# Last row of layer 2: its normalising factor by a square root on ScalarE and a reciprocal on VectorE instead of a power on GpSimd

## The chip, the cores and the metric

One core of one Trainium2 chip. The metric is the device time of one execution of the kernel in microseconds; lower is better. Engines are named as in the profile: PE is TensorE's matmul, PEld its weight load, DVE VectorE, ACT ScalarE, POOL GpSimd, SP SyncE, which here only issues transfers. A "q" behind an engine's name is its instruction queue.

## The reference

Four residual layers on one sequence of 2048 rows of 576 numbers, in float32. Layers A mix by discrete Fourier transforms, written as products with given cosine and sine matrices; layers B gate the layer-normed rows with a long convolution that does not depend on `x`.

```python
def _layernorm(x, axis=-1, eps=1e-5):
    m = jnp.mean(x, axis=axis, keepdims=True)
    v = jnp.var(x, axis=axis, keepdims=True)
    return (x - m) / jnp.sqrt(v + eps)

def _A_ref(x, dft_seq_re, dft_seq_im, dft_hid_re, dft_hid_im):
    a = jnp.einsum("bsd,ed->bse", x, dft_hid_re)
    b = jnp.einsum("bsd,ed->bse", x, dft_hid_im)
    return jnp.einsum("ts,bse->bte", dft_seq_re, a) - jnp.einsum("ts,bse->bte", dft_seq_im, b)

def _B_ref(q, k, v, shift_k, ssm_k, ssm_D):
    ...            # short convolution of k, times v, long convolution by FFT: y
    return q * y

x = A_x
x = x + _A_ref(_layernorm(x, axis=-1), A_dft_seq_re, A_dft_seq_im, A_dft_hid_re, A_dft_hid_im)
x = x + _B_ref(_layernorm(x, axis=-1), B_k, B_v, B_shift_k, B_ssm_k, B_ssm_D)
x = x + _A_ref(_layernorm(x, axis=-1), A_dft_seq_re, A_dft_seq_im, A_dft_hid_re, A_dft_hid_im)
x = x + _B_ref(_layernorm(x, axis=-1), B_k, B_v, B_shift_k, B_ssm_k, B_ssm_D)
```

## The kernel before, in words

The 2048 rows lie as 16 tiles of 128 partitions by 576 numbers; the code calls one tile a row `j`, from 0 to `J - 1` = 15. Every float32 product is made of products of rounded halves: `split` (lines 97 to 99) writes the rounded half on ScalarE (line 98) and the remainder on VectorE (line 99).

A layer A first multiplies by the sequence matrices, streamed in from memory block by block, then by the 576x576 hidden matrices (`hidden`, lines 276 to 289). The first pass of the kernel also computes the long convolution of layer B once, beside TensorE's work, and stores it in `yb_d`. The second pass saves matmuls over the sequence matrices by a Strassen scheme (`strassen`, lines 952 to 1008). The very last stage is the loop at lines 1066 to 1074: for each of four blocks and each of the four rows in it, `hidden` runs two halves of 288 columns of 27 matmuls each, adds each half to the residual (line 287), and then calls `done1` (lines 735 to 744), which does the last layer B and sends the row out.

`done1` uses `gated` (lines 656 to 670). It loads the convolution's row, gets mean and variance through `norm_stats` (lines 177 to 185), forms (x − mean) · y on VectorE (line 665), multiplies by the factor and adds the residual (line 668). `norm_stats` takes the statistics of two halves (line 181), joins them (line 182), adds epsilon (line 183) and raises to the power −0.5 on GpSimd (line 184). For the last row alone, `last` is given: line 668 then runs in two halves of 288 columns, and the first half is sent by ScalarE's queue, the second by SP's (line 739). The other rows are sent whole by SP (line 744).

Small numbers live in the tile `flts`: the constant −0.5 in column 0 (`mhalf`), and four `stat` slots of 20 columns that are used in turn. Line 175 is a first activation on ScalarE, in front of all work. Some rows of the first pass and the second layer take their statistics by `sums` (lines 646 to 654), with a Copy and a Square on ScalarE instead of line 181.

The order of instructions on an engine is laid out when the kernel is built, from the program and its dependences; in places the source fixes it with `tc.issue_after` (`behind`, lines 102 to 106). So it need not be the source's order: `f1_loads` (line 416) stands in the source ahead of the first split in `f1_split`.

Of the kernel before, what the change touches and what calls it, by code (L numbers as in the profile page):

```python
# [12 lines left out]
AF = mybir.ActivationFunctionType  # L13
OP = mybir.AluOpType
# [8 lines left out]
HD = D // 2  # L23
NC = 4
REM = D - NC * P
EPS = 1e-5
# [39 lines left out]
def fnet_h3_kernel(ctx: ExitStack, tc: tile.TileContext, x, c_mat, w_re, w_im, k_pad, v, shift_k,  # L66
                   ssm_k, ssm_d, f1c, i2c, midc, out):
    nc = tc.nc
# [43 lines left out]
    def flat(words, dt, name):  # L112
        return sb.tile([P, words], dt, tag=name, name=name)
# [15 lines left out]
    ring = {}  # L129

    def lay(t, at, *sizes):

        for name, words, n in sizes:
            ring.setdefault(name, Ring()).tiles.extend(t[:, at + i * words:at + (i + 1) * words] for i in range(n))
            at += n * words
        assert at <= t.shape[1], (at, t.shape, sizes)
        return at
# [16 lines left out]
    um = []  # L154

    flts = flat(FLT, F32, "flts")
    mhalf = flts[:, :1]
    lay(flts, 8, ("stat", STAT, 4))
    lay(flts, RT_AT, ("rt", NT, 1))
    lay(mats, X_END, ("cs", WIDE, 3))  # L160
# [5 lines left out]
    def load_after(dst, src):  # L166
        with tc.issue_after(anchor[-1]):
            return nc.sync.dma_start(dst, src).ins
# [3 lines left out]
            nc.gpsimd.dma_start(dst, src)  # L172

    nc.vector.memset(mhalf, -0.5)
    nc.scalar.activation(flts[:, 1:2], mhalf, AF.Copy)

    def norm_stats(src):
        m = ring["stat"]()
        st, mv, ve, rs = m[:, :12].rearrange("p (a c) -> p a c", a=2), m[:, 12:14], m[:, 14:15], m[:, 15:16]
        for i in range(2):  # L180
            nc.vector.bn_stats(st[:, i, :], src[:, i * HD:(i + 1) * HD])
        nc.vector.bn_aggr(mv, st)
        nc.vector.tensor_scalar(ve, mv[:, 1:2], EPS, None, op0=OP.add)  # L183
        pows.append(nc.gpsimd.tensor_tensor(rs, ve, mhalf, OP.pow).ins)  # L184
        return mv, rs, m[:, 16:17]
# [460 lines left out]
    def sums(src, junk):  # L646
        m = ring["stat"]()
        sm, sv, rs, nb = (m[:, i:i + 1] for i in range(4))
        nc.scalar.activation(junk, src, AF.Copy, accum_out=sm)
        nc.vector.tensor_scalar(sm, sm, -1.0 / D, None, op0=OP.mult)  # L650
        nc.scalar.activation(junk, src, AF.Square, bias=sm, accum_out=sv)
        nc.vector.tensor_scalar(sv, sv, 1.0 / D, EPS, op0=OP.mult, op1=OP.add)
        pows.append(nc.gpsimd.tensor_tensor(rs, sv, mhalf, OP.pow).ins)
        return sm, rs, nb

    def gated(xa, q, j, junk=None, last=None):
        load_after(q, yb_d[j])
        if junk is None:
            mv, rs, _ = norm_stats(xa)
            mean, op = mv[:, 0:1], OP.subtract  # L660
        else:
            mean, rs, _ = sums(xa, junk)
            op = OP.add
        yield
        nc.vector.scalar_tensor_tensor(q, xa, mean, q, op0=op, op1=OP.mult)
        for i in range(2 if last else 1):
            cs = slice(i * HD, (i + 1) * HD) if last else slice(None)
            nc.vector.scalar_tensor_tensor(q[:, cs], q[:, cs], rs, xa[:, cs], op0=OP.mult, op1=OP.add)
            if last:
                last(i, cs)  # L670

# [35 lines left out]
    def make_x1(j):  # L707
        xa, q = ring["xa"](), ring["yb"]()
        load_after(xa, xa_d[j])
        for _ in gated(xa, q, j, ring["xj"]() if j % 2 and j >= EARLY else None):  # L710
            yield
        for _ in normed_x(q, xa, ring["xj"]()):
            to_store.append((xb_d[j], q))
            yield
        to_store.append((y_d[j // 2][:, j % 2, :], xa))
        X[j] = to_x(xa, j)
        ready.add(j)
# [17 lines left out]
    def done1(j, xa):  # L735
        q = ring["yb"]()

        def store(i, cs):
            (nc.scalar if i == 0 else nc.sync).dma_start(out[:, j, cs], q[:, cs])

        for _ in gated(xa, q, j, last=store if j == J - 1 else None):
            pass
        if j < J - 1:
            nc.sync.dma_start(out[:, j, :], q)
# [27 lines left out]
    for n, whole in layer(get_x0, lambda j: x[:, j, :], done0, pending):  # L772
# [30 lines left out]
        m = n - PREP  # L803
# [138 lines left out]
    cs, done = {}, []  # L942
# [212 lines left out]
```

## Time and profile before

| | |
|---|---|
| median of 3 runs | 1190.23 us |
| the three runs | 1188.69, 1190.23, 1192.36 us |
| the profiled execution: time / span | 1191.32 / 1189.5 us |
| mean granted TensorE clock | 0.998 |
| busy share of the span | PE 98%, DVE 73%, ACT 55%, POOL 6% |
| power on GpSimd, line 184 | 35 times, 0.547 to 1.055 us, the last at 1183.3 us |

The profile shows one execution. The span is the time from its first to its last instruction; the device time contains some more around it. In rows of the timeline the first number is the start, the second the duration, both in us, then engine, line, operation, what is written and read, and the shape; a bracket gives the idle time of the engine before and what ended it. In rows of groups, the numbers behind the first bar are the summed busy time in us and the mean of one in ns, those behind the second the idle time before them.

### The profile page before, as it was taken

The page shows a single profiled execution, that of the slowest core. Times are in us where ns is not written, and L with a number is a line of the kernel's source. Part 1 is how long each engine was busy: PE and PEld are TensorE (multiplying, and loading weights), DVE is VectorE, ACT ScalarE, POOL GpSimd, SP SyncE. Part 2 cuts the span into 40 slices and gives each one's busy share as a digit, 9 for nine tenths or more (in the row PEclk, how much of TensorE's full clock was granted, in tenths as well). Part 3 has the DMA queues.
Part 4 walks back from the last instruction along what each step waited for, and adds up shares of the span by engine and source line. Part 5 has one row for each costly group of instructions (what it writes and reads, how often), then busy time and mean ns, then how long its engine had stood idle before and what let it go on. Part 6 is the DMA issues. An engine that isn't in the chain of part 4 may idle for free.

```text
span 1189.5 us, 18071 instructions
## 1 busy us (share of the span) xinstructions
PE 1168.5 (98%) x6184; PEld 987.2 (83%) x6184; DVE 872.8 (73%) x1562; ACT 650.0 (55%) x1279; POOL 75.1 (6%) x116
## 2 busy tenths in 40 slices
PE   7999999999999999999999999999999999999997
PEld 5776767888888888888888898888888888889997
DVE  7899983688777778787767665865776776775764
ACT  7865555567766668766645666534444445450200
POOL 2210000000000000001101111000000000001111
PEclk9999999999999999999999999999999999999999
DMA  9869898545656656648966777772772776795621
GB/s 340 295 197 306 269 290 267 178 139 177 225 189 198 200 160 204 186 137 239 273 197 226 235 246 231 251 250 73 255 248 71 240 273 248 266 322 158 214 83 41
DMA packets 147454, 255.65 MB, mean 215 GB/s; under 512 B 16161, under 2 KB 56353, under 8 KB 147362
## 3 DMA queue, kind: packets, MB, share of 16 engines
q1 hardware_dynamic: 111890, 210.17, 54.9%
q10 hardware_dynamic: 28560, 37.91, 9.1%
q0 software_dynamic: 6912, 6.43, 2.4%
q8 instruction: 48, 0.79, 0.3%
q14 instruction: 44, 0.36, 0.1%
HBM read 187.80 MB, written 66.65 MB: 214 GB/s over the span
## 4 chain that ended last, share of the span: by engine, by line
PE 76%; ACT 2%; DVE 2%; DMA 2%; issue 1%; POOLq 0%; ACTq 0%; DVEq 0%
PE s L75 42%; PE bk L75 29%; PE rm L75 4%; ACT flts L512 1%; ACT mid L512 1%; DMA t<-ud 1%; DVE mid L518 0%; DMA yb<-flts 0%; DMA flts<-vd 0%; DMA flts<-in_c_mat 0%; DVE flts L532 0%; DVE flts L530 0%; ACT u L98 0%; DVE flts L531 0%; DVE flts L533 0%
## 5 line engine op out<-in xcount | busy, mean ns | idle before, releaser
L75 PE MATMUL s<-mats 128*128 128x512 f32 x2088 | 543.0, 395 | 1.6 <-ACT mats L195 0.8
L75 PEld LDWEIGHTS s<-mats 128*128 128x128 f32 x2088 | 381.0, 188 | 83.2 <-issue 10.6
L99 DVE TENSOR_TENSOR mats<-flts,mats 128x512 fp32r<-128x512 f32 x206 | 141.0, 688 | 50.8 <-ACT mats L98 48.4
L98 ACT ACTIVATE mats<-flts 128x512 fp32r<-128x512 f32 x206 | 128.3, 628 | 82.6 <-PE bk L75 31.2
L75 PE MATMUL bk<-mid 128*128 128x288 f32 x704 | 127.7, 302 | 1.6 <-DVE flts L287 0.8
L75 PEld LDWEIGHTS bk<-mid 128*128 128x128 f32 x704 | 108.0, 188 | 23.7 <-ACT flts L512 5.8
L512 ACT ACTIVATE flts<-bk 128x288 f32<-128x288 f32 (+1 forms) x192 | 76.3, 406 | 90.8 <-PE bk L75 75.9
L75 PE MATMUL bk<-w,u 128*128 128x288 f32 x864 | 121.3, 296 | 1.0 <-DVE w L241 0.4
L75 PEld LDWEIGHTS bk<-w,u 128*128 128x128 f32 x864 | 117.3, 188 | 5.5 <-DVE flts L532 1.7
L518 DVE TENSOR_TENSOR mid<-flts,mid 128x576 fp32r<-128x576 f32 (+1 forms) x149 | 93.4, 629 | 18.6 <-ACT mid L512 15.2
L75 PE MATMUL rm<-mats 128*128 128x512 f32 x304 | 94.6, 391 | 0.2 <-ACT flts L512 0.2
L512 ACT ACTIVATE mid<-flts 128x576 fp32r<-128x576 f32 (+1 forms) x148 | 80.3, 575 | 11.8 <-DVE flts L533 8.5
L287 DVE TENSOR_TENSOR flts<-flts,bk 128x288 f32<-128x288 f32 x48 | 21.8, 453 | 65.8 <-PE bk L75 65.7
L451 ACT ACTIVATE flts<-bf 128x384 f32<-128x384 f32 (+1 forms) x104 | 43.2, 463 | 46.0 <-PE bf L75 45.9
L75 PE MATMUL bk<-mats 128*128 128x288 f32 (+1 forms) x376 | 67.8, 317 | 0.0
L75 PEld LDWEIGHTS rm<-mats 128*128 128x128 f32 x304 | 56.9, 188 | 12.8 <-ACT flts L512 0.6
L75 PE MATMUL s<-t,mats 128*128 128x512 f32 x264 | 65.4, 390 | 0.6 <-DVE t L99 0.3
L184 POOL TENSOR_TENSOR flts<-flts 128x1 f32<-128x1 f32 x35 | 28.7, 821 | 522.4 <-DVE flts L183 522.3
L75 PE MATMUL bk<-mats,t 128*128 128x288 f32 (+1 forms) x368 | 59.3, 303 | 0.0
L512 ACT ACTIVATE flts<-flts 64x288 f32<-64x288 f32 x128 | 56.6, 443 | 4.7
L75 PEld LDWEIGHTS s<-t,mats 128*128 128x128 f32 x264 | 49.4, 188 | 11.7 <-DVE t L99 0.8
L75 PEld LDWEIGHTS bk<-mats 128*128 128x128 f32 x376 | 55.5, 188 | 3.4
(146 smaller groups left out, 1496.7 us busy)
## 6 DMA issues: line engine op xcount, KB each, us to landing
flts<-in_c_mat SPq DMA_DIRECT2D x148, 256.0 KB, 3.3
ph<-in_c_mat SPq DMA_DIRECT2D x54, 512.0 KB, 4.5
flts<-in_c_mat SPq DMA_DIRECT2D x30, 512.0 KB, 4.8
flts<-td SPq DMA_DIRECT2D x53, 288.0 KB, 2.9
td<-flts ACTq DMA_DIRECT2D x36, 384.0 KB, 4.6
vd<-flts ACTq DMA_DIRECT2D x64, 144.0 KB, 2.7
flts<-vd SPq DMA_DIRECT2D x32, 288.0 KB, 4.1
ud<-ph ACTq DMA_DIRECT2D x12, 512.0 KB, 6.3
```

What stands on the lines that cost most here:

```text
L75: return nc.tensor.matmul(ps, lhsT, rhs, start=first, stop=last, skip_group_check=more).ins
L98: a = nc.scalar.activation(h, src, AF.Copy).ins
L99: return a, nc.vector.tensor_tensor(l, src, h.bitcast(F32), OP.subtract).ins
L184: pows.append(nc.gpsimd.tensor_tensor(rs, ve, mhalf, OP.pow).ins)
L287: added[:] = [nc.vector.tensor_tensor(r[:, cs], r[:, cs], ps[:, :HD], OP.add).ins]
L451: stored[:] = [nc.scalar.activation(so[:, i, :], ps[i], AF.Copy).ins]
L512: last_act.append(nc.scalar.activation(*args, **kw).ins)
L518: nc.vector.tensor_tensor(l, src, h.bitcast(F32), OP.subtract)
```

## The change

For the last row of layer 2 alone, `gated` no longer calls `norm_stats`. It takes the same statistics on VectorE, then ScalarE computes the square root of the variance plus epsilon, the latter as a 128x1 bias operand; after line 665's product VectorE computes the reciprocal, and the two halves of line 668 use it as before. Epsilon is a new constant in `flts`, set by a memset at the start, and the first activation of the kernel becomes a square root of that constant instead of a copy of −0.5. All other rows keep the power on GpSimd.

```diff
-    mhalf = flts[:, :1]
+    mhalf, eps = flts[:, :1], flts[:, 2:3]
...
     nc.vector.memset(mhalf, -0.5)
-    nc.scalar.activation(flts[:, 1:2], mhalf, AF.Copy)
+    nc.vector.memset(eps, EPS)
+    nc.scalar.activation(flts[:, 1:2], eps, AF.Sqrt)
...
         load_after(q, yb_d[j])
-        if junk is None:
+        if last:
+            m = ring["stat"]()
+            st, mean, var = m[:, :12].rearrange("p (a c) -> p a c", a=2), m[:, 12:13], m[:, 13:14]
+            for i in range(2):
+                nc.vector.bn_stats(st[:, i, :], xa[:, i * HD:(i + 1) * HD])
+            nc.vector.bn_aggr(m[:, 12:14], st)
+            rs, op = m[:, 14:15], OP.subtract
+            nc.scalar.activation(var, var, AF.Sqrt, bias=eps)
+        elif junk is None:
             mv, rs, _ = norm_stats(xa)
             mean, op = mv[:, 0:1], OP.subtract
         else:
...
         nc.vector.scalar_tensor_tensor(q, xa, mean, q, op0=op, op1=OP.mult)
+        if last:
+            nc.vector.reciprocal(rs, var)
         for i in range(2 if last else 1):
             cs = slice(i * HD, (i + 1) * HD) if last else slice(None)
-            nc.vector.scalar_tensor_tensor(q[:, cs], q[:, cs], rs, xa[:, cs], op0=OP.mult, op1=OP.add)
+            nc.vector.scalar_tensor_tensor(q[:, cs], q[:, cs], rs, xa[:, cs],
+                                           op0=OP.mult, op1=OP.add)
```

## The prediction

> **What bounds the kernel now.** I read the profile page first, then the timeline of the last eight microseconds, then the waits there, then the first six microseconds, because the edit touches only these two ends.
>
> ```profile
> span 1189.5 us, 18071 instructions
> PE 1168.5 (98%) x6184; PEld 987.2 (83%) x6184; DVE 872.8 (73%) x1562; ACT 650.0 (55%) x1279; POOL 75.1 (6%) x116
> ...
> PE 76%; ACT 2%; DVE 2%; DMA 2%; issue 1%; POOLq 0%; ACTq 0%; DVEq 0%
> ```
>
> TensorE is busy for 1168.5 of 1189.5 us and carries 76% of the chain that ended last; all other engines together are a few per cent of it. So an edit away from TensorE counts only where TensorE has nothing left to do. The last row of layer 2 is such a place. Its timeline (start, duration, engine, line; the last row is a DVE-only piece of the merged pair above it):
>
> ```profile
> 1181.43 0.29 PE L75 MATMUL bk<-mats 128*128 128x288 f32 x1
> 1181.77 0.45 DVE L287 TENSOR_TENSOR ph<-ph,bk 128x288 f32<-128x288 f32 x1 [2.65 <-PE bk L75]
> 1182.26 0.46 DVE L181 BATCH_NORM_STATS2 flts<-ph 128x6 f32<-128x288 f32 x1
> 1182.75 0.21 DVE L182 BATCH_NORM_AGGREGATE flts<-flts 128x2 f32<-128x12 f32 x1
> 1182.99 0.15 DVE L183 TENSOR_SCALAR flts<-flts 128x1 f32<-128x1 f32 x1
> 1183.06 0.81 DVE L665 SCALAR_TENSOR_TENSOR ph<-ph,flts 128x576 f32<-128x576 f32 x1
> 1183.29 0.99 POOL L184 TENSOR_TENSOR flts<-flts 128x1 f32<-128x1 f32 x1 [6.17 <-DVE flts L183]
> 1184.31 0.95 DVE L668 SCALAR_TENSOR_TENSOR ph<-ph,flts 128x288 f32<-128x288 f32 x2 [0.44 <-POOL flts L184]
> 1184.86 0.39 ACTq L739 DMA_DIRECT2D out<-ph  x1
> 1185.29 0.33 SPq L739 DMA_DIRECT2D out<-ph  x1
> ...
> 1184.75 0.51 DVE L668 SCALAR_TENSOR_TENSOR ph<-ph,flts 128x288 f32<-128x288 f32 x1
> ```
>
> The last matmul ends at 1181.72. From there one chain runs to the end: residual add L287, statistics L181 and L182, epsilon L183, the power L184 on GpSimd, and the two halves of L668. L665 needs only the mean and runs beside the power. The bracket on L668 is the reader's point: VectorE had finished L665 (1183.06 + 0.81 = 1183.87) and stood idle 0.44 us for L184. This is the whole prize: nothing before 1182.96 changes, and L668 cannot start before L665 has ended. Behind it the shape stays: half 0 is sent by ScalarE's queue at 1184.86, half 1 by SP's at 1185.29, and the rest of the span is the transfer and the kernel's end.
>
> **The change part by part.** *Removed on the path:* L183 and L184. *Added:* a square root on ScalarE after L182, with epsilon as its bias, and a reciprocal on VectorE after L665. Neither operation is in this trace, so I price them from the nearest rows: by form (mean ns after the bar's first number), then the first instructions of the kernel, then two hand-overs between VectorE and ScalarE and two neighbours on VectorE.
>
> ```profile
> L191 ACT ACTIVATE early<-early,flts 128x576 f32<-128x576 f32 x8 | 6.9, 858 | 0.0
> L651 ACT ACTIVATE early<-early,flts 128x576 f32<-128x576 f32 x8 | 6.2, 772 | 1.4 <-DVE flts L650 0.7 <-DVE flts L675 0.6
> L649 ACT ACTIVATE early<-early 128x576 f32<-128x576 f32 x8 | 5.4, 678 | 0.0
> ...
> 0.74 1.28 ACT L175 ACT_TABLE_LOAD   x1 [0.74 <-PEq L1147]
> 0.81 0.06 DVE L174 MEMSET flts<- 128x1 f32 x1 [0.81 <-PEq L1147]
> 2.04 0.20 ACT L175 ACTIVATE flts<-flts 128x1 f32<-128x1 f32 x1
> 3.64 0.82 DVE L181 BATCH_NORM_STATS2 flts<-early 128x6 f32<-128x288 f32 x2 [2.77 <-DMA early<-in_x]
> 4.35 0.68 ACT L98 ACTIVATE f1r<-flts 128x576 fp32r<-128x576 f32 x1 [2.11 <-DMA flts<-in_ssm_k]
> 5.43 0.42 ACT L416 ACTIVATE f1r<-f1f 128x256 fp32r<-128x256 f32 x1 [0.40 <-DMA f1f<-in_f1c]
> ...
> 659.43 0.16 DVE L650 TENSOR_SCALAR flts<-flts 128x1 f32<-128x1 f32 x1 [0.24 <-ACT gate L649]
> 659.62 0.78 ACT L651 ACTIVATE gate<-gate,flts 128x576 f32<-128x576 f32 x1 [0.22 <-DVE flts L650]
> 660.30 0.18 ACT L651 ACTIVATION_READ_ACCUMULATOR gate<-gate,flts 128x1 f32 x1
> 660.52 0.15 DVE L652 TENSOR_SCALAR flts<-flts 128x1 f32<-128x1 f32 x1 [0.94 <-ACT gate L651]
> ...
> 635.32 0.68 DVE L198 TENSOR_TENSOR mats<-flts,mats 128x512 fp32r<-128x512 f32 x1
> 635.92 0.81 DVE L665 SCALAR_TENSOR_TENSOR gate<-gate,flts 128x576 f32<-128x576 f32 x1
> ...
> L652 DVE TENSOR_SCALAR flts<-flts x29: 139/154/155, 28.9 to 733.8; 128x1 f32<-128x1 f32 x29
> L190 DVE TENSOR_SCALAR flts<-flts x8: 157/211/215, 5.6 to 25.5; 128x1 f32<-128x1 f32 x8
> ```
>
> *The square root.* A 128x1 activation took 0.20 us (2.04, no pointer operand). L651 takes its bias from a 128x1 operand and L649 has none: 772 − 678 = 94 ns, the function aside. So about 0.29 us; the ends are 0.20 and 0.38, the latter with a second pointer as in L191 (858 − 678 = 180 ns more). The hand-over from VectorE to ScalarE is 659.62 − 659.59 = 0.03 us, and back 660.52 − 660.48 = 0.04 us. L182 ends at 1182.96, so the root runs from 1182.99 to 1183.28 and its result can be used from 1183.32.
>
> *L665.* It moves into L183's place, 1182.99 instead of 1183.06, and ends at 1183.80. So it covers the whole root: VectorE is free for the reciprocal from about 1183.72, 0.40 us after the root can be used. If that cover were gone, each further microsecond of the root would be paid in full.
>
> *The reciprocal.* It reads 128x1 and writes 128x1; the nearest rows are L652 at 0.154 us (29 of them alike) and, upwards, L190 at 0.211; downwards the memset at 0.06. I take 0.15, since most one-input 128x1 rows lie there. It does not need L665's result, so it may start before that one ends, as L665 at 635.92 did 0.08 before L198's end at 636.00: 1183.72 to 1183.87. L668 depends on it. Dependent neighbours lie 0.03 apart (L182 ends 1182.96, L183 starts 1182.99), so L668 starts at 1183.90 instead of 1184.31: **0.41 us earlier**. What is late next is VectorE's own queue.
>
> *Ends of this sum.* Best case, the reciprocal disappears under L665: 1183.80 + 0.03 = 1183.83, a gain of 0.48. Worst case of the rows, it starts only behind L665 and costs 0.21: 1183.83 + 0.21 + 0.03 = 1184.07, a gain of 0.24.
>
> *Queues.* The reciprocal makes VectorE wait for ScalarE; queued behind it are only the two L668, and behind those the two output transfers. On ScalarE nothing but the transfer of half 0 stands behind the root, and the engine is otherwise empty there:
>
> ```profile
> 1132.02 0.63 ACT L938 ACTIVATE mats<-mats 64x512 fp32r<-64x512 f32 x1
> ```
>
> After this row ScalarE's next entry is the issue at 1184.86. No transfer changes queue, size or number.
>
> *The head.* One more memset of 0.06 us, in front of VectorE's 2.77 us of idleness before 3.64. The first activation becomes a root that waits for it, but the table load holds ScalarE until 2.02 anyway, and ScalarE then idles 2.11 us before 4.35. Cost nothing; were that idleness gone, 0.06 us.
>
> *Sum.* The profiled execution took 1191.32 us, 1.82 over its span, so it becomes 1190.91. It lay 1.09 above the median of the runs; on the median, 1190.23 − 0.41 = **1189.82 us**. That is 0.03%. The three runs lie from 1188.69 to 1192.36, so a measurement can hardly tell less than 0.3% (3.57 us) from no change.
>
> **The rivals.**
>
> *B, a second and third table load.* One ACT_TABLE_LOAD serves Copy (L649), Square (L651) and Identity (L191) in the whole run. If the set that holds the root lacks one of these, a load of 1.28 us comes early and another before the last root. Early, it costs 0 (in the idle 2.11 before 4.35) to 1.28. In the tail, if the load starts only with the root, the root ends at 1182.99 + 1.28 + 0.29 = 1184.56, and L668 starts 0.04 + 0.15 + 0.03 later, at 1184.78: 0.47 later than now. Together up to +1.75, 1191.98 us: slower than before. The tail turns into a loss once the root ends after 1184.09, that is 1.10 us after L182's hand-over. Against it: ScalarE is idle from 1132.65, so a load without a wait would be over long before. Chance 6%.
>
> [...]
>
> *C, another order of the instructions.* The order on an engine is not the source's: L98 at 4.35 runs ahead of L416 at 5.43, though the source has L416 first. An order made by a planner could shift anywhere when two instructions at the head and four at the end change.
>
> ```profile
> L99 DVE TENSOR_TENSOR mats<-flts,mats 128x512 fp32r<-128x512 f32 x206 | 141.0, 688 | 50.8 <-ACT mats L98 48.4
> L98 ACT ACTIVATE mats<-flts 128x512 fp32r<-128x512 f32 x206 | 128.3, 628 | 82.6 <-PE bk L75 31.2
> ```
>
> Each split of a matrix block that lands late for TensorE costs 0.63 + 0.69 = 1.32 us. It takes three in series to leave the 0.3%: 1189.82 + 3.95 = 1193.8, or as much the other way, 1185.9. Against it: both engines wait for transfers at 3.64 and 4.35, after the changed head is over. Chance 7%, 4 slower and 3 faster.
>
> *D, a reciprocal that works in several passes.* [...] Chance 3%. [...] No row here shows a reciprocal.
>
> *E, the change does not shorten the path.* If L668 waits for something else that also ends near 1184.3, 1190.2 us. The waits name nothing but L184. Chance 3%.
>
> **How the numbers follow.** The forecast has 81%. Shifting the three runs by −0.41 gives 1188.28 to 1191.95; the best end of the sum (−0.48) takes the low end to 1188.2, rival B's 1191.98 the high end to 1192.0. Only C and the odd run lie outside. The forecast, B, D and E all lie within 0.3%; C gives 4% slower and 3% faster, and I add 2% to each for the spread of the runs: faster 0.05, same 0.89, slower 0.06.
>
> **What would show it.** Right: no L184 in the last row, a root of 0.2 to 0.4 us beside L665, a reciprocal of about 0.15 us directly behind it, no idle time above 0.05 us before L668, the 4.24 us from L668's end at 1185.26 to the span's end as they were, so that the time from the last matmul to L668's start falls from 2.59 to about 2.18 us. Exactly one table load. Wrong: VectorE idle before the reciprocal and released by ScalarE (B), a reciprocal near 1 us (D), or TensorE's idle time away from the last 8 us changed by microseconds (C).

## The result and the profile after

| | before | after |
|---|---|---|
| median of 22 runs each | 1190.45 us | 1188.95 us |
| ratio of the times, after to before | | 0.9984, 95% interval 0.9979 to 0.9990 |
| profiled execution: time / span | 1191.32 / 1189.5 us | 1188.28 / 1186.4 us |

The changed kernel is faster by 1.2 to 2.5 us. The forecast was 0.41 us: the time lies in its range and within its 0.3%, but the gain is three to six times the forecast one.

The timeline of the changed kernel's last row (start, duration, engine, line):

```profile
1177.23 2.56 PE L75 MATMUL bk<-mats 128*128 128x288 f32 x18
1179.83 0.45 DVE L288 TENSOR_TENSOR ph<-ph,bk 128x288 f32<-128x288 f32 x1 [2.65 <-PE bk L75]
1180.32 0.46 DVE L663 BATCH_NORM_STATS2 flts<-ph 128x6 f32<-128x288 f32 x1
1180.81 0.21 DVE L664 BATCH_NORM_AGGREGATE flts<-flts 128x2 f32<-128x12 f32 x1
1181.06 0.30 ACT L666 ACTIVATE flts<-flts 128x1 f32<-128x1 f32 x1 [49.30 <-DVE flts L664]
1181.06 0.82 DVE L674 SCALAR_TENSOR_TENSOR ph<-ph,flts 128x576 f32<-128x576 f32 x1
1181.79 0.16 DVE L676 RECIPROCAL flts<-flts 128x1 f32<-128x1 f32 x1
1181.98 0.95 DVE L679 SCALAR_TENSOR_TENSOR ph<-ph,flts 128x288 f32<-128x288 f32 x2
1182.53 0.39 ACTq L751 DMA_DIRECT2D out<-ph  x1
1182.96 0.33 SPq L751 DMA_DIRECT2D out<-ph  x1
```

Lines 665 and 668 of before are 674 and 679 here, 287 is 288. The two halves of line 668 (679 here) are called the products from here on. From the start of the last residual add to the start of the products it was 1184.31 − 1181.77 = 2.54 us and is 1181.98 − 1179.83 = 2.15: 0.39 less. But to the span's end it was 1189.50 − 1181.77 = 7.73 and is 1186.39 − 1179.83 = 6.56: **1.17 less**. (The views print the span and the starts of a queue's entries to 0.1 us. Where a finer figure stands here for one of them, it is from the trace's records, which carry nanoseconds.) Another 0.78 us went away behind the last product, where the change has no instruction. What runs there are the queues' own entries at the kernel's end, listed under the closing line of the program; DRAIN and EVENT_SEMAPHORE are the trace's names for two kinds of them. For the kernel before (least, median and greatest duration in ns, then first and last start in us):

```profile
L1151 SPq EVENT_SEMAPHORE  x12: 17/28/28, 1185.7 to 1189.4; - x12
L1151 POOLq EVENT_SEMAPHORE  x4: 17/17/17, 1188.3 to 1189.4; - x4
L1151 POOLq DRAIN  x3: 45/241/5019, 1183.3 to 1189.2; - x3
L1151 SPq DRAIN  x3: 7/7/7, 1187.5 to 1188.5; - x3
```

And for the kernel after:

```profile
L1163 SPq EVENT_SEMAPHORE  x12: 17/28/28, 1183.3 to 1186.3; - x12
L1163 POOLq EVENT_SEMAPHORE  x4: 17/17/17, 1185.2 to 1186.3; - x4
L1163 POOLq DRAIN  x3: 93/193/5021, 1174.2 to 1186.0; - x3
L1163 SPq DRAIN  x3: 7/7/7, 1185.1 to 1185.4; - x3
```

Read the first starts together. SP's closing entries wait for the landings of the two output transfers, as the view of SP's waits says (before, then after):

```profile
SPq L1151 <- DMA out<-ph: 1.2, 2, 0.9
...
SPq L1163 <- DMA out<-ph: 1.2, 2, 0.9
```

SP's first DRAIN marks that it is through: 1187.5 before, 1185.1 after. GpSimd has a DRAIN of 5.02 us that is under way when its last power starts: before, at 1183.26 against 1183.29, the last row's power. So it ended at 1183.26 + 5.02 = 1188.28, and GpSimd's next entry, the semaphore at 1188.3, came 0.8 us after SP was through. With that semaphore the closing round begins, the exchange of semaphores among all engines that takes the last 1.2 us. After, the last power is that of the row ahead, at 1174.2, whose DRAIN was over by 1179.2; the closing round begins at 1185.2, right behind SP. Before, the kernel's end waited for GpSimd; after, it waits for SP, and so for the last transfer. So far this is a reading of two profiles; the experiments test it.

### The profile page after: what moved, and what is told of

The parts are those of the page before. It is cut to its first block, busy times and chain, and to the rows that moved or that the text cites. A ratio compares the mean times of both kernels' runs of the same rounds, so it can differ in the third digit from the quotient of the medians.

```text
span 1186.4 us, 18071 instructions
## 1 busy us (share of the span) xinstructions
PE 1167.3 (98%) x6184; PEld 986.3 (83%) x6184; DVE 872.3 (74%) x1563; ACT 650.2 (55%) x1280; POOL 74.7 (6%) x115
## 4 chain that ended last, share of the span: by engine, by line
PE 75%; ACT 2%; DVE 2%; DMA 1%; issue 1%; ACTq 0%; DVEq 0%; SPq 0%
PE s L75 42%; PE bk L75 29%; PE rm L75 4%; ACT flts L513 1%; ACT mid L513 1%; DVE mid L519 1%; DMA t<-ud 1%; DMA flts<-td 0%; DMA flts<-vd 0%; DVE flts L533 0%; ACT mats L98 0%; DMA vd<-flts 0%; DVE flts L532 0%; DVE flts L531 0%; DVE flts L534 0%
```

## The experiments

Three theories went in. *Drain*: the above; the later of the last landing and GpSimd's DRAIN ends the kernel. *Wait*: the prediction's; only the products' start counts. *Head*: the new first instructions shift something in the long stages. The table has what each profile shows, in us after the start of the last residual add, in one execution each, from the trace's records: the start of the products, SP's first DRAIN, the end of GpSimd's long DRAIN and the span's end. One execution is enough for differences of tenths here: the two profiles of the changed kernel have their end at 6.559 and 6.562, and before and *head alone*, which have the same last row, at 7.728 and 7.740. The ratio is to the kernel before, from 11 runs (after: 22), with its 95% interval.

| kernel | products | SP through | GpSimd drained | end | ratio |
|---|---|---|---|---|---|
| before | 2.54 | 5.7 | 6.52 | 7.73 | 1 |
| after | 2.15 | 5.3 | ahead | 6.56 | 0.9984 (0.9979 to 0.9990) |
| after again | 2.16 | 5.3 | ahead | 6.56 | 0.9988 (0.9980 to 0.9997) |
| power kept | 2.18 | 5.3 | 5.83 | 6.89 | 0.9996 (0.9987 to 1.0005) |
| power late | 2.15 | 5.3 | 7.73 | 8.80 | 1.0012 (1.0003 to 1.0021) |
| head alone | 2.55 | 5.7 | 6.52 | 7.74 | 1.0000 (0.9991 to 1.0009) |
| products late, no power | 2.46 | 5.6 | ahead | 6.87 | 0.9993 (0.9984 to 1.0002) |
| multiplication late | 2.15 | 5.3 | 7.38 | 8.47 | one run |
| three powers late | 2.16 | 5.3 | 8.99 | 10.14 | one run |
| copy late | 2.15 | 5.3 | 7.35 | 8.45 | one run |

**After again.**

> The changed kernel once more, as it is. Three theories. Drain: the kernel's end waits for GpSimd's queue to drain, which lasts until 5.02 us after the start of its last power; with the last row's power gone, this leaves the end of the kernel, and the time from the last matmul's end to the span's end falls from 7.78 to 6.61 us: about 1.2 us faster than before. Wait: only the wait of line 668 is shortened, 0.40 us; all else is the spread of single executions, so 0.4 us faster. Head: the new first instructions shift work of the long stages too, so 1.5 to 1.9 us faster, with 0.3 to 0.7 of it ahead of the last matmul.

The time from the add to the end came out the same to 0.01 us. The ratio's interval, 0.4 to 2.4 us faster, holds Drain's 1.2 and the Head's 1.5 to 1.9, and just reaches Wait's 0.4, which the first result's interval (1.2 to 2.5) leaves out. Times alone do not part Drain and Head here; the next runs do.

**Power kept**, unread, beside the root:

```diff
-            nc.scalar.activation(var, var, AF.Sqrt, bias=eps)
+            root = m[:, 15:16]
+            nc.scalar.activation(root, var, AF.Sqrt, bias=eps)
+            nc.gpsimd.tensor_tensor(m[:, 16:17], var, mhalf, OP.pow)
...
-            nc.vector.reciprocal(rs, var)
+            nc.vector.reciprocal(rs, root)
```

> The changed kernel, and beside the square root a power of the variance on GpSimd that nobody reads. Drain: the power starts about 1.4 us after the last matmul's end, the queue is drained 5.02 later at 6.4, and the span ends 1.2 behind that: 7.6 us from the last matmul to the end, 1.0 us slower than the changed kernel and 0.2 faster than the kernel before, although line 668's products start as early as in the changed kernel. Wait and Head: nobody waits for this power, so 6.6 us from the last matmul to the end, as in the changed kernel.

The products start at 2.18, nobody waits for the power, and the end comes 0.33 us later than in the changed kernel (6.89 against 6.56). From its timeline:

```profile
1181.28 0.84 DVE L676 SCALAR_TENSOR_TENSOR ph<-ph,flts 128x576 f32<-128x576 f32 x1
1181.32 0.55 POOL L668 TENSOR_TENSOR flts<-flts 128x1 f32<-128x1 f32 x1 [5.92 <-DVE flts L664]
```

And its closing entries:

```profile
L1165 POOLq EVENT_SEMAPHORE  x4: 17/17/17, 1185.9 to 1186.8; - x4
L1165 POOLq DRAIN  x3: 45/93/4591, 1181.3 to 1186.7; - x3
L1165 SPq DRAIN  x3: 7/7/7, 1185.4 to 1186.1; - x3
```

SP is through at 1185.4, GpSimd's DRAIN at 1181.29 + 4.59 = 1185.88, and the closing round starts at 1185.9. Drain has the direction, and 1.0 us was too much for it: this power took 0.55 us instead of 0.99, and the DRAIN was shorter by just that, 4.59 against 5.02. The rest is a power that started 0.09 us earlier than reckoned and a closing round shorter by 0.15 (1.07 us from the DRAIN's end to the span's end, 1.21 before). So not 5.02 us from the start is the constant, but what lies behind the computation's end. In the records the DRAIN starts a little ahead of the power, by 0.027 us before and 0.035 here, so this is 5.019 − 0.986 − 0.027 = 4.006 and 4.591 − 0.549 − 0.035 = 4.007: **4.01 us** in both. The expectations of the last four runs call it 4.04, which takes DRAIN and power to start together. Wait and Head have no reason for any delay.

**Power late**, unread, behind the last product:

```diff
+        if last:
+            nc.gpsimd.tensor_tensor(m[:, 16:17], rs, q[:, D - 1:D], OP.pow)
```

> The changed kernel, and behind the last product a power on GpSimd, which nobody reads and which takes one column of that product as its exponent. Drain: it starts about 3.3 us after the last matmul's end, the queue is drained at 8.3, the span ends at 9.5: 2.9 us slower than the changed kernel and 1.7 slower than the kernel before. Wait and Head: a power of 0.55 to 1 us ends at 4.3, before the output transfers have landed at 5.4, so nothing is lost: 6.6 us.

This makes the term large, and it shows in the times as well: 0.4 to 2.5 us slower than the kernel before, though the products start as early as in the changed one. The end lies 8.80 − 6.56 = 2.24 us later; Drain's 2.9 was reckoned with a power of 0.99, and this one took 0.55 (0.44 less), started 0.08 us earlier than reckoned and had a closing round 0.15 us shorter. Wait and Head, which saw no loss, fall. From its timeline, then its closing entries:

```profile
1181.24 0.94 DVE L679 SCALAR_TENSOR_TENSOR ph<-ph,flts 128x288 f32<-128x288 f32 x2
...
1182.26 0.55 POOL L684 TENSOR_TENSOR flts<-flts,ph 128x1 f32<-128x1 f32 x1 [7.82 <-DVE ph L679]
```

```profile
L1165 POOLq EVENT_SEMAPHORE  x4: 17/17/17, 1186.9 to 1187.8; - x4
L1165 POOLq DRAIN  x3: 45/93/4592, 1182.2 to 1187.6; - x3
L1165 SPq DRAIN  x3: 7/7/7, 1184.4 to 1187.1; - x3
```

SP was through at 1184.4 and the closing round waited until 1186.9, where the DRAIN ended (1182.23 + 4.59 = 1186.82).

**Head alone**: the kernel before with the two changed places at the start.

```diff
-    nc.scalar.activation(flts[:, 1:2], mhalf, AF.Copy)
+    nc.vector.memset(eps, EPS)
+    nc.scalar.activation(flts[:, 1:2], eps, AF.Sqrt)
```

> The kernel before with the head of the change alone: the memset of epsilon and the first activation as a square root. The last row keeps the power and its wait. Drain and Wait: 7.78 us from the last matmul to the end, and the time of the kernel before within 0.3 us. Head: faster than before by the part of the gain that lies ahead of the last matmul, 0.3 to 0.7 us.

It took 7.74 us from the add to the end, at a ratio of 1.0000 (0.9991 to 1.0009). The head is worth nothing that can be seen; up to 1.1 us either way is not excluded by the times. In this kernel and the changed one the instructions start in the same order on TensorE and SP, and on VectorE and GpSimd the order differs in the last row alone. On ScalarE, one activation and one issue of a transfer beside it also change places; such pairs do so between the two profiles of the changed kernel as well.

**Products late, no power**: the DRAIN is out of the way, but the products start nearly as late as before the change.

```diff
+            nc.vector.tensor_tensor(ring['rt']()[:, :HD], xa[:, :HD], q[:, HD:], OP.add)
             nc.vector.reciprocal(rs, var)
```

> The changed kernel with one unread VectorE sum of 128x288 put between the reciprocal and the last products, so that line 668's products start about as late as before the change (some 2.5 us after the last residual add starts), but without a power. Drain, as the first four runs sharpened it: the kernel ends about 1.1 us behind the later of two things, the last transfer's landing or the last GpSimd computation's end plus 4.04 us. Then the last residual add's start to the span's end is 6.57 + 0.38 = 6.95 us, and 0.8 us of the gain over the kernel before stays. Wait: the products start as late as before, so nothing is left of the gain: 7.73 us and the time of the kernel before.

From its timeline:

```profile
1183.27 0.16 DVE L677 RECIPROCAL flts<-flts 128x1 f32<-128x1 f32 x1
1183.39 0.46 DVE L676 TENSOR_TENSOR flts<-ph 128x288 f32<-128x288 f32 x1
1183.77 0.94 DVE L680 SCALAR_TENSOR_TENSOR ph<-ph,flts 128x288 f32<-128x288 f32 x2
```

The sum went behind the reciprocal and the products started at 2.46. The end came at 6.87, 0.86 ahead of the kernel before's and 0.31 behind the changed one's, which is just what the products lost (2.46 − 2.15 = 0.31). Drain's 6.95 fits, but for products that were delayed by 0.31 and not 0.38; Wait's 7.73 does not. With the DRAIN gone, the products' delay counts in full. The times alone (1.9 us faster to 0.2 slower) hold both theories; the verdict rests on the profile.

**Multiplication late, three powers late, copy late**: what the 4.01 us belong to. One execution each; the edit is the late power's, with `OP.mult`, with two more powers `(m[:, 16:17], rs, mhalf)` behind it, or with `nc.gpsimd.tensor_copy(m[:, 16:17], q[:, D - 1:D])` in its place.

> Like the run with the late power, but GpSimd multiplies instead of raising to a power. If the 4.04 us follow any computation of GpSimd: from the last residual add's start to the end about 8.8 us less what the multiplication is shorter than 0.55. If they belong to the power: 6.6 us, as in the changed kernel.

> Like the run with the late power, with two more unread powers behind it. If the 4.04 us count from the last computation's end: two powers of 0.55 more, 8.82 + 1.1 = 9.9 us from the last residual add's start to the end. If they count from the first one, or are a fixed start-up that the first has paid: 8.8 us.

> Like the run with the late power, but GpSimd only copies one column of the last product, with a single input. If the 4.04 us follow any computation of GpSimd: 8.8 us from the last residual add's start to the end, less what the copy is shorter than 0.55. If they belong to the power or to two-input operations: 6.6 us.

For each of the three, in this order, first GpSimd's computations in the timeline, then its DRAIN in the closing entries:

```profile
1186.09 0.19 POOL L684 TENSOR_TENSOR flts<-flts,ph 128x1 f32<-128x1 f32 x1 [7.83 <-DVE ph L679]
```

```profile
L1165 POOLq DRAIN  x3: 45/102/4231, 1186.1 to 1191.1; - x3
```

```profile
1183.70 0.55 POOL L684 TENSOR_TENSOR flts<-flts,ph 128x1 f32<-128x1 f32 x1 [7.83 <-DVE ph L679]
1184.32 1.18 POOL L686 TENSOR_TENSOR flts<-flts 128x1 f32<-128x1 f32 x2
```

```profile
L1167 POOLq DRAIN  x3: 45/152/4592, 1184.9 to 1190.4; - x3
```

```profile
1187.94 0.18 POOL L684 COPY flts<-ph 128x1 f32<-128x1 f32 x1 [7.81 <-DVE ph L679]
```

```profile
L1165 POOLq DRAIN  x3: 45/102/4211, 1187.9 to 1193.0; - x3
```

In the records the DRAIN starts 0.036 us ahead of the multiplication and 0.020 ahead of the copy, so 4.231 − 0.189 − 0.036 = 4.006 and 4.211 − 0.184 − 0.020 = 4.007: both are followed by the same 4.01 us as a power. With three powers the DRAIN begins with the last one (1184.9) and ends at 1184.915 + 4.592 = 1189.507, again 4.01 us after the pair's end at 1185.501. So it is any of these computations of GpSimd, and it counts from the last one. The ends, 8.47, 10.14 and 8.45 against 8.4, 9.9 and 8.4 forecast, agree; two further powers cost 1.34 instead of 1.1, since they took 1.18 and followed with a gap of 0.08, and the closing round was 0.08 us longer.

What the 4.01 us are made of, these runs do not show.

## Why the prediction was right, and where it was too small

- **The path from the last matmul to the products** held, step by step. Root: 0.30 us (0.29 forecast), 0.04 after line 664's end. Reciprocal: 0.16 (0.15), started 0.08 ahead of line 674's end (0.08). Products: 0.03 behind it. In all 0.39 earlier, forecast 0.41. The root's cover by the 128x576 product held as well.
- **"This is the whole prize", "behind it the shape stays" and the 4.24 us from the last product to the span's end** are the step that failed. These 4.24 us (1189.50 − 1185.26) became 3.46 (1186.39 − 1182.93); that they would stay was one of the signs of being right that the prediction named, and it did not hold. I read them as the transfer and a fixed end, but GpSimd's DRAIN stood in them, 0.8 us later than SP was through with the transfers. The trace of before had it: a POOLq DRAIN of 5019 ns starting at 1183.3. The prediction rested on the page and the timeline, which do not list such entries of a queue; those of the program's closing line would have shown it. The chain that ended last, in order of time, names an entry of that line as well, beside the power; its 1.02 us are the part of the DRAIN up to the power's end:

```profile
1183.26 1.02 POOLq L1151
```

- So the sum was mis-sized by its missing term: 0.78 us of DRAIN beside 0.39 of wait, 1.17 in all. The two do not simply add. While a power runs that late, earlier products are hidden behind its DRAIN: *power kept* has them at 2.18, and its end at 6.89 is still set by GpSimd at 5.83, not by SP at 5.3. And with the DRAIN gone but the products at 2.46, the end is 6.87, set by SP.
- **The time itself** fell into the forecast range because the range is wide, not because the sum was complete: it was laid out from three runs that spread over 3.7 us, so any gain up to 2 us on their median lies in it.
- **Rival E's** premise, that something else ends late beside the power, was nearly this, but I looked for it ahead of the products and priced it as no gain.
- **Rival B** is out: one load, as before, in the groups of the changed kernel by line:

```profile
L176 ACT ACT_TABLE_LOAD x1 | 1.3, 1283 | 0.7 <-PEq L1159 0.7
```

  This load of 1283 ns at 0.7 us served the root and every other activation. Why the root needs no load of its own, the trace does not show.
- **Rival D** is out: 156 ns for the reciprocal, against 154 for a 128x1 row of line 652. No run shows a reciprocal that works in several passes, to which I gave 3%; at one element a partition this one took 2 ns longer than a row of line 652.
- **Rival C**: the order differs only in the last row and by the one memset, apart from the neighbours on ScalarE named under *head alone*. The last residual add began at 1181.77 in the profile of before and 1179.83 in that of after, 1.94 us of the 3.1 by which the two spans differ. I do not count that as the change's: in the other executions with the changed head it lay anywhere from 1179.08 to 1184.78.
- **What stays open:** a gain of 1.17 us is a ratio of 0.9990 on 1190.45, the upper edge of the first interval (0.9979 to 0.9990) and inside the second (0.9980 to 0.9997). Whether a further few tenths come from elsewhere, these runs do not settle.

## What to carry to other kernels

The end of this kernel was a race between queues, not only between computations (before, SP was through at 1187.5 us, GpSimd's DRAIN at 1188.28): list each engine's closing entries, and see which DRAIN or landing comes last, before pricing an edit near the end. Here each GpSimd computation that was tried, a plain copy of 0.18 us too, had to end 4.01 us ahead of the closing round, or the kernel waited for it; so in a kernel like this keep GpSimd out of the last few microseconds, and hand the last small step to ScalarE or VectorE, as here the root of 0.30 us and the reciprocal of 0.16. Taking away a wait paid only as far as the next queue: without GpSimd's DRAIN, products 0.31 us later cost 0.31 us; in *power kept* GpSimd was through over 0.4 us behind SP, so the early products could not show. No run moved the products with the DRAIN in place.

## What the runs showed of the hardware that I had not expected

- GpSimd's queue needed 4.01 us (4.005 to 4.007 in the records of these runs) from the end of its last computation until its DRAIN was over, for a power of 0.99 us, a power of 0.55, a multiplication of 0.19 and a copy of 0.18.
- The same 128x1 power took 0.99 us where it started 0.23 us after the start of a 128x576 product on VectorE (1183.29 against 1183.06), and 0.55 where it started 0.04 after the start of one (1181.32 against 1181.28) or with VectorE idle (1182.26). These runs do not show the reason.
